# Strassen's algorithm for four of the seven pairs of token tiles in the last product of an attention and MoE kernel

## The chip, the cores and the metric

The kernel runs on one core of a Trainium2 chip. The metric is the time of one execution on the device, in microseconds (us). A core has TensorE (matrix products, PE in the profile, with its weight loads as PEld), VectorE (DVE), ScalarE (ACT) and GpSimd (POOL), each with its own row of instructions; SyncE (SP) and some of the others issue DMA transfers. An engine works its row off in order and waits, where it must, on semaphores.

## The reference, cut to what matters

```python
def _attn_ref(q, k, v, w_pre, w_post):           # 4 batches, 12 heads, 448 x 64
    scores = np.matmul(q, k.transpose(0, 1, 3, 2)) / np.sqrt(64)
    ...                                          # heads mixed, softmax, heads mixed
    return np.matmul(attn, v)

def _moe_ref(x, w_in, w_out, g_ln):              # x 1792 x 768, w_in 768 x 1024, w_out 1024 x 768
    h = x @ w_in
    e = np.exp(h - np.max(h, axis=-1, keepdims=True))
    solu = h * (e / (np.sum(e, axis=-1, keepdims=True) + 1e-9))
    mu = np.mean(solu, axis=-1, keepdims=True)
    var = np.mean((solu - mu) ** 2, axis=-1, keepdims=True)
    ln = (solu - mu) / np.sqrt(var + 1e-06) * g_ln
    return ln @ w_out
```

The result of the attention, 1792 token rows of 768, is x. The weights w_in and w_out come as fp64.

## The kernel before

The attention part fills the first 441 us or so and leaves x transposed in DRAM and, for the last batch, in SBUF. The change doesn't touch it. Then comes the part around the MoE layer, to which all that follows belongs. It works on 14 tiles of 128 token rows. Every factor of a product is held as two fp16 numbers, a higher and a lower half, and a product is three matmuls: high by high, high by low, low by high.

For each tile t:

- `hidden` (L984) is h = x @ w_in: 36 matmuls of 128x512, three products by six blocks of the inner dimension by two halves of the 1024 columns. The result lies in a pair of PSUM banks, `ps_h`, of which there are three (tile t uses number t modulo 3). The last batch's three tiles come first, from xsh and xsl, then those from xf0, xf1 and xf2, which SyncE loads from DRAM (L870, L872).
- On VectorE `solu_max` (L1508), on ScalarE `solu_exp` (L1519), on VectorE two steps on one column (`sm`, L1530 and L1533) and `solu_product` (L1536), behind which the bank pair is free for `hidden` of tile t + 3.
- The layer norm: `ln_mean` (nmu, L1547, VectorE), `ln_square` (L1552, ScalarE), `ln_var` (v, L1558, VectorE), `ln_root` (L1563, GpSimd, a power of -0.5), `ln_newton` in four small steps on VectorE (z, z again, rs, nm: L1568, L1571, L1574, L1578), `ln_apply` (L1584, GpSimd), and the split into a higher half `lh` (`ln_hi`, L1590, ScalarE) and a lower one `ll` (`ln_lo`, L1594, GpSimd).
- `turn` (L1598): SyncE issues two DMA transposes, from `lh` and `ll` in SBUF to `lth` and `ltl`, with nine slots each.
- `project` (L1609) is y = ln @ w_out: 48 matmuls of 128x384, eight blocks of the inner dimension by three products by two halves of the columns; each half has a PSUM bank. Tile 13 has 512 and 256 columns instead.
- `emit` (L1621, ScalarE) brings y to SBUF, and `stores` (L1765) go out on SyncE.

Beside the `hidden` tiles w_out is made ready. For each of its eight blocks of 128 rows SyncE fetches 768 KB of fp64 into one of two conversion buffers (`cv_wo`, L883), and six steps turn it into fp32: VectorE L898, ScalarE L901, VectorE L904, L909 and L914, GpSimd L917. ScalarE takes each block's maximum (`w_out_max`, L1478). When all eight are there, VectorE multiplies them with g (am_o, L1484) and reduces them; two matmuls on TensorE (`spread_wo`, L332) bring the maximum to all partitions; VectorE reduces it (L342), makes a power of two of it (L306 to L318) and `gs_wo` and `c_out` (L1490, L1491). Then ScalarE makes the eight higher halves `wo_h` (L360) and VectorE the eight lower ones `wo_l` (L365).

What stands where in an engine's row is decided by a planner: every piece of work is added with its engine and a cost, what it comes after, a due time and, if it takes a buffer, the ring of that buffer and what frees it. `moe.order()` then lists the pieces, by due times and modelled costs. `hidden` of tile t is due at 7.75 (t - 1), w_out's block kc at 9.0 kc, and `project` of tile t lags eleven tiles behind its `hidden`. In the list that results, TensorE's row is `hidden` 0 to 12, `project` 0, `hidden` 13, `project` 1 to 13.

Of the kernel before, what the change touches and what calls it, by code (L numbers as in the profile page):

```python
# [240 lines left out]
def kernel(  # L241
# [49 lines left out]
    E_S, E_X, E_LN = 19, 17, 10  # L291
# [1109 lines left out]
    with tc.manual_schedule():  # L1401
# [22 lines left out]
        lt_p = ctx.enter_context(tc.tile_pool(name="lt", bufs=9))  # L1424
# [20 lines left out]
        junk = wt_p.tile([128, DFF], F32, name="junk")  # L1445
# [20 lines left out]
        def fetch_w_out(kc):  # L1466
            fetch64(w_out[kc * 128 : (kc + 1) * 128], cv_p, "cv", DM, f"wo{kc}")
# [148 lines left out]

        def emit(t, n):
            if n == 0:
                outs[t] = h_p.tile([128, DM], F32, tag="o", name=f"o_{t}")
            c = slice(*ENDS[t][n : n + 2])  # L1620
            nc.scalar.activation(out=outs[t][:, c], in_=ys.pop((t, n)), func=AF.Copy, scale=c_out)  # L1621
# [12 lines left out]
        one = lambda f, *a: lambda e: f(*a)  # L1634
        add(("zf",), factors, {"dve": 2.2}, due=0.0)
        add(("zg",), lambda e: nc.sync.dma_start(out=g_sb, in_=g_ln.rearrange("(k p) -> p k", p=128)), {"sp": 0.6}, due=3.0, dma=(8, 4, 1))
        for kc in range(KFF):
            due = 9.0 * kc
# [6 lines left out]
                ring="cv",  # L1645
# [4 lines left out]
            on = ({"dve": 0.8}, {"act": 0.9}, {"dve": 1.25}, {"dve": 0.65}, {"dve": 1.35}, {"pool": 1.85})  # L1650
            for i in range(6):
# [6 lines left out]
                    due=due + 1.2 * i,  # L1658
                )
# [143 lines left out]
```

## Time and profile before

| | us |
|---|---|
| median of three runs (650.32 to 654.32) | 653.25 |
| span of the profiled execution | 657.9 |
| TensorE busy in it | 632.8 |
| VectorE busy | 475.1 |
| ScalarE busy | 451.0 |
| GpSimd busy | 280.1 |

The profiled execution is one run, recorded by instruction, and somewhat longer than the median. A busy time is the sum over the engine's instructions, overlaps counted once. An instruction's duration includes what it loses to another that it collides with, but not its wait for semaphores, which is the idle time before it. Times in the rows count from the start of the span.

### The profile page before, as it was taken

The numbers are of one execution on the slowest core, as the hardware profiler recorded it, in microseconds if no ns is written. First come the engines' busy times: TensorE is split into PE (matmuls) and PEld (weight loads), VectorE is DVE, ScalarE is ACT, GpSimd is POOL, SyncE is SP. The second block draws the span as 40 slices with busy tenths as digits, with TensorE's granted clock in tenths as the row PEclk, the third lists the DMA queues.
The fourth block names the chain that finished last, engine by engine and source line by source line (L and its number), as shares of the span: only waits on it lengthen the run. The fifth ranks groups of instructions, "written<-read, shape, count | busy, mean of one in ns | idle before, by whom it ended". The sixth has DMA issues, their size and how long they took to land.

```text
span 657.9 us, 17741 instructions
## 1 busy us (share of the span) xinstructions
PE 632.8 (96%) x6660; PEld 433.7 (66%) x6660; DVE 475.1 (72%) x1314; ACT 451.0 (69%) x981; POOL 280.1 (43%) x427
## 2 busy tenths in 40 slices
PE   6889999999999999999899999999999999999997
PEld 6647767777767778778677777774444455666664
DVE  5769998879997689997699999849889896100000
ACT  4679888989888898988799997725455576311111
POOL 2025683235844254593254246404666846300000
PEclk9779999999999999999899999999999999999999
DMA  9037578467677448788746763019964422541211
GB/s 242 12 133 229 178 152 178 156 196 221 204 185 169 150 140 236 234 175 206 219 154 221 214 224 119 3 41 295 186 160 112 97 48 57 113 113 51 64 55 48
DMA packets 114029, 98.53 MB, mean 150 GB/s; under 512 B 69604, under 2 KB 104600, under 8 KB 113944
## 3 DMA queue, kind: packets, MB, share of 16 engines
q1 hardware_dynamic: 108120, 83.62, 45.8%
q0 software_dynamic: 4416, 12.40, 6.9%
q10 hardware_dynamic: 1408, 1.38, 0.8%
q8 instruction: 52, 0.85, 0.5%
q14 instruction: 33, 0.27, 0.1%
HBM read 33.24 MB, written 9.63 MB: 65 GB/s over the span
## 4 chain that ended last, share of the span: by engine, by line
PE 64%; DVE 17%; ACT 7%; DMA 4%; issue 3%; POOL 2%; SPq 1%; ACTq 0%; DVEq 0%; POOLq 0%
PE y L1609 17%; PE po L766 15%; PE ps_h L984 12%; PE px L815 7%; PE ps L644 6%; PE pm L711 6%; DVE dead L721 4%; DVE s L661 3%; ACT e L737 3%; ACT s L656 2%; DMA raw_q<-in_q_dram 2%; DVE hl_k L365 1%; ACT p_t L369 1%; DMA sr<-s 1%; DMA cv_wi<-in_moe_w_in_dram 1%
## 5 line engine op out<-in xcount | busy, mean ns | idle before, releaser
L766 PE MATMUL po<-wr,e 128*112 128x120 f32 x1440 | 176.0, 273 | 6.4 <-POOL wr L758 4.9
L766 PEld LDWEIGHTS po<-wr,e 128*112 128x112 f32 x1440 | 156.8, 178 | 36.8 <-POOL wr L758 15.9
L758 POOL TENSOR_SCALAR wr<-wq,sm 128x120 f32<-128x120 f32 x180 | 77.1, 436 | 186.1 <-DVE sm L752 90.6
L737 ACT ACTIVATE e<-pm,nb,c_exp 128x448 f32<-128x448 f32 x180 | 131.4, 734 | 19.6 <-DVE dead L721 10.2
L721 DVE TENSOR_SCALAR_CACHE_REDUCE dead<-pm,c_nexp 128x448 f16<-128x448 f32 x180 | 121.7, 676 | 14.1 <-PE pm L711 10.1
L661 DVE SCALAR_TENSOR_TENSOR s<-ps,s 120x448 f16<-120x448 f32 (+1 forms) x192 | 112.2, 615 | 16.1 <-ACT s L656 13.8
L369 ACT COPY p_t<-po 112x480 f32<-112x480 f32 x180 | 108.2, 625 | 13.7 <-PE po L766 12.3
L656 ACT ACTIVATE s<-ps 120x448 f16<-120x448 f32 (+1 forms) x192 | 97.3, 552 | 18.1 <-PE ps L644 17.5
L815 PE MATMUL px<-p_t,raw_v 112*64 112x120 f32 (+3 forms) x1632 | 86.8, 259 | 0.8 <-ACT e L737 0.7
L815 PEld LDWEIGHTS px<-p_t,raw_v 112*64 112x64 f32 x1632 | 76.1, 137 | 16.0 <-issue 11.4
L984 PE MATMUL ps_h<-wi,xf 128*128 128x512 f16 x396 | 86.0, 379 | 0.2 <-DVE u L1536 0.2
L644 PE MATMUL ps<-k,q 64*64 64x448 f16 (+2 forms) x1008 | 79.7, 359 | 2.2 <-DVE s L661 1.5
L1609 PE MATMUL y<-wo_h,lth 128*128 128x384 f16 (+2 forms) x224 | 73.0, 326 | 0.0
L1609 PE MATMUL y<-wo_l,lth 128*128 128x384 f16 (+2 forms) x224 | 73.0, 326 | 0.0
L1609 PE MATMUL y<-wo_h,ltl 128*128 128x384 f16 (+2 forms) x224 | 73.0, 326 | 0.0
L984 PEld LDWEIGHTS <-xf 128*128 128x128 f16 x396 | 38.8, 98 | 46.8 <-issue 0.4
L1621 ACT ACTIVATE o<-y,c_out 128x384 f32<-128x384 f32 (+2 forms) x28 | 16.2, 579 | 72.7 <-PE y L1609 72.7
L1609 PEld LDWEIGHTS <-lth 128*128 128x128 f16 x448 | 43.8, 98 | 29.3
L711 PE MATMUL pm<-sr,wp_hi 64*64 64x448 f16 x720 | 57.1, 363 | 4.4 <-DMA sr<-s 2.4
L644 PEld LDWEIGHTS <-q 64*64 64x64 f16 (+2 forms) x1008 | 34.7, 107 | 24.4 <-issue 8.0
L1594 POOL TENSOR_TENSOR ll<-u,lh 128x1024 f16<-128x1024 f32 x14 | 31.4, 2245 | 15.1 <-ACT lh L1590 9.0
L737 ACT ACTIVATION_READ_ACCUMULATOR e<-pm,nb,c_exp 128x1 f32 x180 | 37.6, 209 | 0.0
(182 smaller groups left out, 800.1 us busy)
## 6 DMA issues: line engine op xcount, KB each, us to landing
sr<-s SPq DMA_DIRECT2D x176, 210.0 KB
cv_wi<-in_moe_w_in_dram SPq DMA_DIRECT2D x24, 256.0 KB
cv_wo<-in_moe_w_out_dram SPq DMA_DIRECT2D x8, 768.0 KB
raw_k<-in_k_dram POOLq DMA_DIRECT2D x18, 224.0 KB, 3.7
raw_q<-in_q_dram POOLq DMA_DIRECT2D x18, 224.0 KB, 5.4
raw_v<-in_v_dram POOLq DMA_DIRECT2D x18, 224.0 KB, 3.8
xh<-xsh SPq DMA_DIRECT2D x9, 224.0 KB
xl<-xsl SPq DMA_DIRECT2D x9, 224.0 KB
```

The lines of the kernel that those rows point to most:

```text
L369: nc.scalar.copy(out=out, in_=in_)
L644: nc.tensor.matmul(sps[b, c, h + e][lo:hi], q2[b, g][rows, 2 * j + x, i0 + lo : i0 + hi], k1[b, g][rows, 2 * j + y], start=(a == 0), stop= ...
L656: nc.scalar.activation(out=s_t[b, c][0 : y.shape[0], h, 0], in_=y, func=AF.Copy, scale=2.0**-E_S)
L661: nc.vector.scalar_tensor_tensor(out=t[:, h, 1], in0=y, scalar=2.0**-E_S, in1=t[:, h, 0], op0=ALU.mult, op1=ALU.subtract)
L711: nc.tensor.matmul(pmx[b, u + i][64 * e : 64 * e + 64, 0:S], w[rows], sr[b, u][rows, e, z], start=(a == 0), stop=(a == 2),)
L721: nc.vector.tensor_scalar(out=dead, in0=pmx[b, u][:, 0:S], scalar1=c_nexp[0:UK, b : b + 1], scalar2=None, op0=ALU.mult, op1=ALU.min, accum ...
L737: nc.scalar.activation(out=ee[b, u], in_=pmx.pop((b, u))[:, 0:S], func=AF.Exp, bias=nbs.pop((b, u)), scale=c_exp[0:UK, b : b + 1], accum_o ...
L758: ENG[eng].tensor_scalar(out=w, in0=wq[0:UK, 0 : H * UN], scalar1=sm, scalar2=1.0, op0=ALU.mult, op1=ALU.mult)
L766: nc.tensor.matmul(ps[:, c * 120 : (c + 1) * 120], e[:, c * CP : (c + 1) * CP], w, start=True, stop=True)
L815: nc.tensor.matmul(xps[b, blk, g][e * 64 : e * 64 + 64, i, cut], raws["v", b, p][:, e, c * D : (c + 1) * D], next(x for y, x in block_view ...
L984: nc.tensor.matmul(ps[:, n], xx[:, kc, o : o + 128], ww[:, kc, n * 512 : (n + 1) * 512], start=(kc == 0 and a == 0), stop=(kc == KDM - 1 a ...
L1609: nc.tensor.matmul(ys[t, n], lts[t, x][:, kc], w[:, kc, c0:c1], start=(kc == 0 and a == 0), stop=(kc == KFF - 1 and a == 2),)
```

## The change

The rows of the layer norm go through DRAM: `lh` and `ll` of a tile are stored there (L1662) and read back by a transposing DMA (L1674) into one tile `lt` per pair of token tiles. Such a pair tile has two slots of its own; two more are the places of xf1 and xf2, when `hidden` no longer reads these. All of y's products stand behind the last `hidden`. Pairs 0, 1 and 2 are computed as before, four results of 24 matmuls of 128x384. Pairs 3 to 6 use Strassen's algorithm in the form with few additions: the two tiles, the two halves of the inner dimension and the two halves of w_out's columns make a 2 x 2 by 2 x 2 product, which takes seven block products of 12 matmuls of 128x384 instead of eight. Their operands are sums and differences. Those of w_out are made once: it is scaled in place in fp32 (eight steps, ScalarE), `w_out_sum` (16 steps of 128x384, VectorE), and new halves `tz` in a former conversion buffer. Those of ln are made for each pair: `pair_whole` (two steps of 128x1024, VectorE, higher plus lower half in fp32, in the place of xf0 or of a raw buffer), `pair_sum` (four of 128x512, VectorE), `part_hi` (two of 128x1024, ScalarE), `part_lo` (two of 128x1024, VectorE). The seven products of a pair go in turn to six half banks of the three `ps_h` pairs, and `emit` adds them up: one step on ScalarE and nine on VectorE, of 128x384 from PSUM. A plain pair's `emit` runs on ScalarE or VectorE.

Also: the small steps nmu, v, the second z and nm move to ScalarE for all tiles; `junk`, into which `ln_square` writes, is fp16; the conversion of w_out has four buffers (two `cv`, two `sz`) and is due at 8.0 kc; the powers of two of ln and w_out change so that sums fit fp16; output stores go out on SyncE or on ScalarE's queue, from three buffers.

```diff
-    E_S, E_X, E_LN = 19, 17, 10
+    E_S, E_X, E_LN = 19, 17, 8
...
-        moe = Plan(h=3, u=3, lh=2, ll=2, th=9, tl=9, cv=2, X=1, Y=1, o=2)
+        moe = Plan(h=3, u=3, lh=2, ll=2, R=2, lt=2, x0=1, x1=1, x2=1, sz=2, B=6, tt=1, cv=2, X=1, Y=1, o=3)
...
+        def w_out_sum(k, i, eng):
...
+            b11, b12, b21, b22 = (raw_of(x)[:, n * DH : (n + 1) * DH] for x in (k, k + KH) for n in range(2))
+            out, x, y = ((t[:, 0], b12, b11), (t[:, 1], b22, t[:, 0]), (b21, b21, t[:, 1]), (b12, b22, b12))[i]
+            minus(eng, out, x, y)
...
-        def turn(t, z):
-            lts[t, z] = lt_p.tile([128, KFF, 128], F16, tag=f"t{z}", name=f"lt{z}_{t}")
-            nc.sync.dma_start_transpose(out=lts[t, z], in_=lns[t, z])
+        def ln_store(t, z, e):
+            QUEUE[e].dma_start(out=ln_dr["hl".index(z)][t], in_=lns[t, z])
...
+            nc.sync.dma_start_transpose(out=lts[i][:, z, t], in_=ln_dr[z][2 * i + t])
...
+        def pair_sum(i, j, eng):
+
+            a11, a12, a21, a22 = (xs[i][:, n] for n in range(4))
+            out, x, y, op = (
+                (a22, a21, a22, ALU.add),
+                (a21, a11, a21, ALU.subtract),
+                (a11, a22, a11, ALU.subtract),
+                (a12, a12, a11, ALU.subtract),
+            )[j]
+            ENG[eng].tensor_tensor(out=out, in0=x, in1=y, op=op)
...
+                y = ys[i, j] = bank(i, j)
+                terms = [(operand(i, j, z, k), factor(j, k)[n]) for k in range(KH) for z, n in ((0, 0), (0, 1), (1, 0))]
...
+            if j == 0:
+                nc.scalar.activation(out=px, in_=y, func=AF.Copy, scale=c_out)
+                return
+            work = {
+                1: lambda: [(py, px)],
+                3: lambda: [(px, px), (py, py)],
+                2: lambda: [(c(0, 0), px)],
+                4: lambda: [(c(1, 1), px), (px, px)],
+                5: lambda: [(c(1, 1), c(1, 1)), (c(1, 0), py)],
+                6: lambda: [(c(0, 1), px)],
+            }
+            for dst, x in work[j]():
+                nc.vector.scalar_tensor_tensor(out=dst, in0=y, scalar=c_out, in1=x, op0=ALU.mult, op1=ALU.add)
...
-            due = 9.0 * kc
+            due = 8.0 * kc
...
-                ring="cv",
+                ring=("cv", "sz")[kc % 4 // 2],
...
-                ("zm", ln_mean, {"dve": (0.08, 0.17)}, 4.1, None, None),
+                ("zm", ln_mean, {"act": (0.19, 0.29)}, 4.1, None, None),
...
-                ("zv", ln_var, {"dve": (0.1, 0.2)}, 5.6, None, None),
+                ("zv", ln_var, {"act": (0.19, 0.29)}, 5.6, None, None),
```

Three places in the new order are shown. The first is TensorE's row where w_out's maximum is spread. Before, the spread matmul stands between the last matmul of `hidden` 11 (bank ps_h_7620) and the first of `hidden` 12 (ps_h_7315):

```order
L984 MATMUL ps_h_7620<-wi_7289,xf_7756 128x512
L984 LDWEIGHTS xf_7756
L984 MATMUL ps_h_7620<-wi_7288,xf_7756 128x512
L332 MATMUL spread_wo<-ident_69,amx_wo 128x128
L984 LDWEIGHTS xf_7756
L984 MATMUL ps_h_7315<-wi_7288,xf_7756 128x512
```

After the change it stands one tile earlier, between `hidden` 10 (ps_h_7622) and `hidden` 11 (ps_h_7623):

```order
L984 MATMUL ps_h_7622<-wi_7289,xf_7774 128x512
L984 LDWEIGHTS xf_7774
L984 MATMUL ps_h_7622<-wi_7288,xf_7774 128x512
L332 MATMUL spread_wo<-ident_69,amx_wo 128x128
L984 LDWEIGHTS xf_7774
L984 MATMUL ps_h_7623<-wi_7288,xf_7774 128x512
```

So TensorE asks for the maximum one `hidden` tile sooner.

The second is VectorE's row at the end of w_out's conversion, up to am_o. Before, with the last conversion step (L914), the small steps of tile 8, and `solu_max` of tiles 9 (ps_h_7315) and 10 (ps_h_7619) around am_o:

```order
L909 TENSOR_SCALAR cv_wo_8288<-cv_wo_8288 128x768
L1558 TENSOR_SCALAR v_8379<-sq_8368,ch 128x1
L914 SCALAR_TENSOR_TENSOR cv_wo_8288<-cv_wo_8288 128x768
L1568 TENSOR_SCALAR z_8386<-y_8382,v_8379 128x1
L1571 TENSOR_SCALAR z_8386<-z_8386 128x1
L1574 TENSOR_SCALAR rs_8426<-z_8386,ch,y_8382 128x1
L1578 TENSOR_SCALAR nm_8430<-nmu_8365,rs_8426 128x1
L1508 TENSOR_SCALAR u_8432,nb_8433<-ps_h_7315,ch 128x1024
L1484 TENSOR_TENSOR am_o<-am_o,g_sb 128x8
L353 TENSOR_REDUCE amx_wo<-am_o 128x1
L1508 TENSOR_SCALAR u_8443,nb_8444<-ps_h_7619,ch 128x1024
```

After it, where L1559 is `solu_max`, L1587 `solu_product`, L1631 and L1637 the z and rs steps, and ps_h_7623 and ps_h_7315 are the banks of tiles 8 and 9:

```order
L909 TENSOR_SCALAR cv_wo_8080<-cv_wo_8080 128x768
L1637 TENSOR_SCALAR rs_8310<-z_8304,ch,y_8296 128x1
L914 SCALAR_TENSOR_TENSOR cv_wo_8080<-cv_wo_8080 128x768
L1631 TENSOR_SCALAR z_8318<-y_8312,v_8308 128x1
L1559 TENSOR_SCALAR u_8320,nb_8321<-ps_h_7623,ch 128x1024
L1637 TENSOR_SCALAR rs_8327<-z_8318,ch,y_8312 128x1
L1581 TENSOR_SCALAR sm_8329<-sm_8329 128x1
L1584 RECIPROCAL sm_8329<-sm_8329 128x1
L1587 SCALAR_TENSOR_TENSOR u_8320,su_8375<-ps_h_7623,sm_8329,u_8320 128x1024
L1559 TENSOR_SCALAR u_8378,nb_8379<-ps_h_7315,ch 128x1024
L1486 TENSOR_TENSOR am_o<-am_o,g_sb 128x8
L353 TENSOR_REDUCE amx_wo<-am_o 128x1
```

The conversion ends a whole `solu_max` and `solu_product` (tile 8's) sooner, the steps on one column are down to z and rs, and am_o no longer has tile 10's `solu_max` in front of the product of tile 9.

The third is SyncE's row in the `y` stage. Before, the transposes of the last tiles alternate with output stores:

```order
L1598 DMA_TRANSPOSE lth_8669<-lh_8561 128x8x128
L1598 DMA_TRANSPOSE ltl_8675<-ll_8572 128x8x128
L1765 DMA out_dram<-o_8623 80x768
L1765 DMA out_dram<-o_8623 48x768
L1598 DMA_TRANSPOSE lth_8818<-lh_8671 128x8x128
L1598 DMA_TRANSPOSE ltl_8823<-ll_8682 128x8x128
```

After it, with lt_8841 the tile of pair 2, lt_8902 of pair 3 and lt_8972 of pair 4:

```order
L1674 DMA_TRANSPOSE lt_8841<-ln_h 128x8x128
L1674 DMA_TRANSPOSE lt_8841<-ln_l 128x8x128
L1662 DMA ln_h<-lh_8893 128x1024
L1674 DMA_TRANSPOSE lt_8902<-ln_h 128x8x128
L1674 DMA_TRANSPOSE lt_8902<-ln_l 128x8x128
L1662 DMA ln_l<-ll_8898 128x1024
L1674 DMA_TRANSPOSE lt_8902<-ln_h 128x8x128
L1674 DMA_TRANSPOSE lt_8902<-ln_l 128x8x128
L2035 DMA out_dram<-o_8890 16x768
L1674 DMA_TRANSPOSE lt_8972<-ln_h 128x8x128
```

The transposes come in fours, a pair's at a time. The first of pair 2 waits until pair 0 is projected, since it takes that pair's slot, and the rest of the row stands behind it.

## Rows read from the trace of the kernel before

**Rows 1.** The page's head: busy us (share of span), instructions.

```profile
span 657.9 us, 17741 instructions
...
PE 632.8 (96%) x6660; PEld 433.7 (66%) x6660; DVE 475.1 (72%) x1314; ACT 451.0 (69%) x981; POOL 280.1 (43%) x427
```

**Rows 2.** Chain of waits, its end: start, us, engine, tile, line, count.

```profile
525.86 1.29 DVE u L1508 x2
...
528.80 7.93 PE ps_h L984 x36
...
544.53 7.77 PE ps_h L984 x36
552.30 101.41 PE y L1609 x624
...
653.73 0.47 ACT o L1621
```

**Rows 3.** TensorE's waits, 441 to 658: total us, times, longest.

```profile
PE ps_h L984 <- DVE u L1536: 0.2, 1, 0.2
```

**Rows 4.** Windows: length, busy PE, PEld, DVE, ACT, POOL; clock, DMA share, GB/s.

```profile
444.39:528.74 84.35, 84.18 (x392) 38.25 (x390) 73.98 (x152) 46.90 (x72) 54.48 (x35) 1.00 0.69 168
448.00:456.00 8.00, 8.00 (x39) 3.61 (x37) 7.41 (x17) 4.14 (x7) 3.88 (x3) 1.00 1.12 320
552.30:653.73 101.43, 101.40 (x624) 60.84 (x622) 6.17 (x20) 20.98 (x34) 10.70 (x8) 1.00 0.28 70
584.50:587.00 2.50, 2.50 (x17) 1.53 (x16) 0.00 (x0) 0.00 (x0) 0.00 (x0) 1.00 1.01 192
653.73:657.90 4.17, 0.00 (x0) 0.00 (x0) 0.00 (x0) 0.47 (x1) 0.00 (x0) 1.00 0.25 59
```

**Rows 5.** Lines, VectorE, 444.39 to 530.87: busy us, mean ns | idle before.

```profile
L1536 DVE SCALAR_TENSOR_TENSOR u<-ps_h,sm,u 128x1024 f32<-128x1024 f32 x11 | 14.1, 1284 | 0.4
L1508 DVE TENSOR_SCALAR_CACHE_REDUCE u<-ps_h,ch 128x1024 f32<-128x1024 f32 x11 | 14.0, 1275 | 0.7 <-PE ps_h L984 0.7
...
L1568 DVE TENSOR_SCALAR z<-y,v 128x1 f32<-128x1 f32 x9 | 2.4, 272 | 3.0 <-POOL y L1563 3.0
L1578 DVE TENSOR_SCALAR nm<-nmu,rs 128x1 f32<-128x1 f32 x9 | 1.9, 214 | 0.3
L1558 DVE TENSOR_SCALAR v<-sq,ch 128x1 f32<-128x1 f32 x9 | 1.9, 207 | 0.9 <-ACT junk L1552 0.8
...
L1547 DVE TENSOR_SCALAR nmu<-su 128x1 f32<-128x1 f32 x10 | 1.5, 148 | 0.2
L1571 DVE TENSOR_SCALAR z<-z 128x1 f32<-128x1 f32 x9 | 1.4, 154 | 0.3
L1484 DVE TENSOR_TENSOR am_o<-am_o,g_sb 128x8 f32<-128x8 f32 x1 | 1.1, 1118 | 0.6 <-ACT cv_wo L1478 0.6
```

**Rows 6.** Timeline of VectorE: start, us, line, operation.

```profile
450.29 0.96 DVE L914 SCALAR_TENSOR_TENSOR cv_wo<-cv_wo 128x768 f32<-128x768 uint32 x1
...
503.47 2.19 DVE L914 SCALAR_TENSOR_TENSOR cv_wo<-cv_wo 128x768 f32<-128x768 uint32 x1
...
530.79 0.61 DVE L342 TENSOR_REDUCE amx_wo<-spread_wo 128x1 f32<-128x128 f32 x2
...
532.34 0.15 DVE L1491 TENSOR_SCALAR c_out<-p_wo 128x1 f32<-128x1 f32 x1
```

**Rows 7.** Lines, all engines, 430 to 658, columns as in Rows 5.

```profile
L365 DVE SCALAR_TENSOR_TENSOR wo_l<-wo,gs_wo,wo_h 128x768 f16<-128x768 f32 x8 | 8.4, 1109 | 0.0
...
L1519 ACT ACTIVATION_READ_ACCUMULATOR u<-ps_h,nb,ch 128x1 f32 x14 | 2.7, 190 | 0.0
```

**Rows 8.** Timeline of SyncE's queue: start, us, line, operation.

```profile
463.43 3.24 SPq L1598 DMA_TRANSPOSE ltl<-ll x1
...
584.70 1.27 SPq L1598 DMA_TRANSPOSE ltl<-ll x1
```

**Rows 9.** The page's costliest groups: busy us, mean ns | idle before.

```profile
L661 DVE SCALAR_TENSOR_TENSOR s<-ps,s 120x448 f16<-120x448 f32 (+1 forms) x192 | 112.2, 615 | 16.1 <-ACT s L656 13.8
```

More of the change, by code (lines that the diff above doesn't have):

```diff
@@ L1617, in emit, with turn @@
[L1617 to L1621, printed above, removed]
+        def ln_store(t, z, e):
+            QUEUE[e].dma_start(out=ln_dr["hl".index(z)][t], in_=lns[t, z])
+        def turn(i, t, z):
+            if i not in lts:
+                n = i - NPL + 1
+                if 0 < n < B - 1:
+                    x = wt_p.tile(x_in[n].shape, F16, tag=f"xf{n}", name=f"lt_{i}")
+                    x = x.rearrange("p z k n -> p (z k n)")[:, 0 : 4 * DFF]
+                else:
+                    x = lt_p.tile([128, 4 * DFF], F16, tag="lt", name=f"lt_{i}")
+                lts[i] = x.rearrange("p (z t k n) -> p z t k n", z=2, t=2, k=KFF)
+            z = "hl".index(z)
+            nc.sync.dma_start_transpose(out=lts[i][:, z, t], in_=ln_dr[z][2 * i + t])
@@ new lines @@
+        T = TP
+        for n, (i, j) in enumerate(STEPS):
+            before = [STEPS[n - 1]] if n else []
+            a, b = 2 * i, 2 * i + 1
+            if i >= NPL:
+                ready = [("zT", i, int(j == 1), z) for z in "hl"] if j < 3 else [("zL2", i, int(j in (4, 5)))]
+                ready += [("zL", x) for x in range(*((0, 4), (12, 16), (4, 8), (8, 12), (8, 12), (16, 20), (4, 8))[j])]
+                ready += [("zp", NT - 1)]
+                ring, until = "B", [("zE", i, j)]
+            else:
+                ready = [("zT", i, PLAIN[j][0], z) for z in "hl"] + [("zL", k) for k in range(KFF)]
+                ring, until = "XY"[j % 2], [("zE", i, j)]
+            add(
+                ("zP", i, j),
+                one(project, i, j),
+                {"pe": TQ if i >= NPL else 2 * TQ},
+                after=ready,
+                behind=[("zP",) + x for x in before] or [("zh", NT - 1)],
+                due=T,
+                ring=ring,
+                until=until,
+            )
+            T += TQ if i >= NPL else 2 * TQ
+            last = i == NPP - 1
+            if i >= NPL:
+                ring = "o" if j in (2, 4) else None
+                t = a + (j == 4)
+                until = [("zO", t, x) for x in chunks(t)]
+                goes = {2: [(a, 0, 1)] if last else [], 5: [(b, 0, 2)], 6: [(a, int(last), 2)]}.get(j, [])
+                on = {"act": (0.45, 0.6)} if j == 0 else {"dve": (1.22, 1.35) if j in (3, 4, 5) else (0.61, 0.75)}
+            else:
+                t = a + PLAIN[j][0]
+                ring = "o" if j < 2 else None
+                until = [("zO", t, x) for x in chunks(t)]
+                goes, on = [(t, 0, 2)] if j > 1 else [], {"act": (0.58, 0.7), "dve": (0.55, 0.7)}
+            add(
+                ("zE", i, j),
+                lambda e, i=i, j=j: emit(i, j, e),
+                on,
+                after=[("zP", i, j)],
+                behind=[("zE",) + x for x in before],
+                due=T - 12,
+                ring=ring,
+                until=until,
+            )
+            for t, c0, c1 in goes:
+                cut = slice(c0 * DH, c1 * DH)
+                for x, (_, d, rows) in enumerate(stores(t, cut)):
+                    add(
+                        ("zO", t, x) + ((c1,) if c1 < 2 else ()),
+                        lambda e, d=d, rows=rows, t=t, cut=cut: QUEUE[e].dma_start(out=d, in_=outs[t][rows, cut]),
+                        {"sp": 0.6, "act": 0.6},
+                        after=[("zE", i, j)],
+                        due=T + 0.7 + 0.1 * x,
```

328 lines of the change are left out of this document (245 added, 83 removed).

## The prediction

> **What bounds the kernel now.** I read the page's head first: TensorE is busy 632.8 of 657.9 us [rows 1]. Then the end of the chain of waits: from 528.80 on it is TensorE alone, and just ahead of that a few VectorE steps stand in it; the waits give TensorE one idle time after 441.41, of 0.2 us, in front of the matmuls at 528.80 [rows 2, 3]. The windows say the same: in the last 101.43 us TensorE is idle for 0.03 us at clock 1.00, and VectorE works 6.17 us [rows 4]. So from 441 on the time is matmuls times their spacing, and other work counts only where it makes TensorE wait. Behind the last matmul lie 4.17 us. Up to the first `hidden` tile both kernels do the same work in the same order; I give that part nothing.
>
> **The sum, part by part.**
>
> *Matmuls.* After the last `hidden` tile 624 matmuls of 128x384 (48 of them cut into 512 and 256 columns, the same sum) take 101.41 us [rows 2], 0.1625 us each; tile 0's 48 lie ahead of that tile. All 14 tiles are 672. After the change three plain pairs take 96 each and four Strassen pairs 7 x 12 = 84 each, 624 in all. 48 go: 48 x 0.1625 = **7.80 us**. Tile and type of the new matmuls are the same, so I use the same spacing; the weight loads (60.84 us in that stretch [rows 4]) stay one to a matmul.
>
> The Trainium skill ("TensorE: Matmul & The Clock Gate", Back-to-back issue gap) says that a sustained stream of weight loads and matmuls settles at about 81 ns for 128 columns and 131 ns for 512, which is an estimate of 114 ns at 384; by it the 48 matmuls would be worth 5.5 us. This trace differs, with 162.5 ns at 384 and 216 ns at 512 (7.77 us for 36 [rows 2]), and the measurement decides.
>
> *The bank wait.* `hidden` 12 waits 0.2 us for tile 9's `solu_product`, because am_o and a `solu_max` stood ahead of it on VectorE [rows 2, 3]. With the conversion of w_out due earlier this goes: **0.2 us**.
>
> *`hidden` stage: does VectorE keep up?* The two spread matmuls of w_out's maximum now stand between `hidden` 10 and 11 instead of 11 and 12. One `hidden` is 7.77 us and `hidden` 11 ended at 528.6, so 10 ends at 520.8: by then am_o must be there. From 444.39 to 528.74 VectorE is busy 73.98 of 84.35 us [rows 4]. Up to am_o in its new place these go: one `solu_max` and one `solu_product` (2.6), nine or ten each of nmu, v, z' and nm, now on ScalarE (1.5 + 1.9 + 1.4 + 1.9), and a z and an rs step (0.5) that fall behind it [rows 5]. 64.2 are left, so am_o is done at 508.6 with no wait at all, and at 519.0 with all of today's 10.4 us of waits. It also stands behind tile 9's `solu_max`, which can't start before `hidden` 9 ends, at 513.0; 1.3 for that and 1.1 for am_o give 515.5 [rows 5, 6]. **Slack 2 to 5 us, cost 0.** Then comes tile 10's product, which must free its bank ahead of `hidden` 13: 520.8, 0.5 for the spread matmuls, 1.7 for the reductions and scale as from 530.79 to 532.49 today, 1.3 for a `solu_max`, six lower halves of w_out at 1.11, 1.1 of small steps, 1.3 for the product [rows 5, 6, 7]: 533.4. `hidden` 13 is due at 520.8 + 0.5 + 2 x 7.77 = 536.8. Slack 3. If that cover goes, each us late is a us.
>
> The small steps have no row on ScalarE; the nearest is its accumulator read of one column, 0.19 [rows 7]. Four a tile at 0.2 add 7 us to ScalarE's 46.90 of 84.35 [rows 4]: not a bound. They may lengthen a tile's chain by tenths, but behind the `solu_product` that TensorE waits for.
>
> *Rows through DRAM.* 28 stores of 256 KB are added on SyncE's queue, and the transposes now read DRAM. In the `hidden` stage this is at most 7.3 MB over 84 us, 87 GB/s beside today's 168; plain loads alone reached 320 [rows 4]. Cost 0.
>
> In the `y` stage SyncE works its instructions off in order. Pair 2's four transposes wait for the slot of pair 0, and pair 3's four stand behind them. Call the end of `hidden` 13 H. Pair 0 takes 96 x 0.1625 = 15.6 us, so they start at H+15.6, and pair 2 needs them at H+31.2. A transpose of today holds the queue for 1.27 us, at worst 3.24, and two of them keep the DMA engines for 2.5 us [rows 4, 8]; those read SBUF, and for DRAM there is no row. With T for one, pair 2 is in time up to T = (15.6 - 2.5) / 4 = 3.3. Pair 3 needs its sums at its fourth step, H+52.7: 8T, 2.5 for a store between and the landing, and 9.0 for two whole sums, four part sums, a cast and two lower halves (1.28, 0.64, 1.28, 1.28 each, worked out below; the cast is assumed as long as a VectorE step) must fit into 37.1 us: T = 3.2, and beyond it TensorE waits 8T - 25.6. I take T = 1.3, today's value where no loads of x or w_out run beside, as in the `y` stage: pair 3 is 15 us early. Cost 0, at the worst row 0.3.
>
> *VectorE in the `y` stage.* It was nearly empty; now it makes operands and recombines. Nearest prices: two-input steps of 768 columns in SBUF at 0.96 and 1.11 [rows 6, 7], so 1.28 to 1.48 for 1024 and 0.64 to 0.74 for 512; a step from PSUM with an added term 0.615 for 448 columns [rows 9], 0.53 for 384, at most 0.66. A Strassen pair has 4, 4 and 9 of these: 12.5 us, at most 14.8. TensorE needs 84 x 0.1625 = 13.65 a pair. Sums and lower halves of w_out add 16, plain emits and the rest of the chains 9. In all 75 us, at most 85, of 101.4; and pair 3's operands are made beside 46.8 us of plain matmuls, so the pairs start with a lead. **Cost 0**; if VectorE paced all four pairs at the bound, 4 x 1.15 = 4.6.
>
> *The end.* Today ScalarE's 0.47 and a store of 256 columns follow the last matmul, 4.17 us together [rows 2, 4]. After: VectorE's 0.53 and a store of 384 columns, on two queues. 0, within 0.5 either way.
>
> Sum: 657.9 - 7.8 - 0.2 = 649.9 us for a profiled run. The median of the runs is 653.25 where this execution has 657.9, so both scale by 0.993: **645.3**.
>
> **The rivals.**
>
> *A. VectorE is late in the `hidden` stage* (slack 2 to 5, and 3). For it: today's 10.4 us of waits may grow with ScalarE's load, and a w_out step that took 0.96 took 2.19 at another place [rows 6]. Against: 10 us of VectorE's work leave. Late by 2 to 6 beyond the slack: 647 to 651.
>
> The Trainium skill ("SBUF — State Buffer", SBUF: two separate sides) has a rule that fits those two rows: a VectorE step with two SBUF inputs and a GpSimd step that reads SBUF shut each other out for a whole instruction. By it the new two-input steps are slow too while GpSimd has work, some 20 us into the `y` stage, where VectorE has its lead.
>
> *B. VectorE paces the Strassen pairs.* For it: 12.5 to 14.8 a pair against 13.65. Against: the lead, and six banks. At the bound 4.6 us are lost: 648 to 650.
>
> *C. Transposes from DRAM are slow.* This ends on the other side: at 8T - 25.6 = 8, T = 4.2, the gain is gone, and at T = 5.0 the kernel is 1% slower; 653 to 662. Against it: the worst row today is 3.24, beside loads that the `y` stage lacks.
>
> *D. The matmuls saved are worth less than their spacing.* At 0.114 each, 647.7. Against: every shape of the stage sits at its spacing.
>
> **How the numbers follow.** Forecast 0.64 (644 to 647), A 0.15, B 0.10, C 0.06, D 0.05. The range from 643 to 651 leaves out most of C, the far ends of A and B (0.07) and an end better than counted (0.04). One per cent, about what a measurement of this kernel can tell from no change, is 6.5 us: under 646.7 is faster. Some 0.53 of the forecast's 0.64 lies there, and 0.02 of A; C and far ends make 0.07 slower; 0.38 lie within.
>
> **What would show it.** Right: 624 `y` matmuls, all behind `hidden` 13, in about 101.4 us, with no wait of TensorE over 0.3; `hidden` 13 ending 8.0 us earlier, since tile 0's `y` no longer stands ahead of it; the spread matmuls don't wait. A: TensorE waits for amx_wo or for tile 10's product. B: `y` of the fifth and later pairs waits for an emit or a lower half. C: the first Strassen pair waits for a transpose or a sum made of one, and SyncE's issues take over 3 us. D: a `y` stage under or over 101.4 us with no wait in it. It would also be wrong by a stall in the attention part, which both share, or by an end that grows by over 1 us.

## The result, and the profile after

| | before | after |
|---|---|---|
| median of four runs, us | 653.39 | 645.72 |
| lowest to highest | 650.32 to 654.32 | 645.40 to 648.39 |
| span of the profiled execution | 657.9 | 644.1 |

The ratio of after to before is 0.9898, with a 95% interval from 0.9869 to 0.9927. The forecast was 645.3. That the number came out almost to the tenth is luck: two terms of the sum were wrong, by 3.5 us together, and the start of the program, which the change doesn't touch, varies from run to run by as much.

The page's head of the kernel after, to be held against [rows 1]:

```profile
span 644.1 us, 17785 instructions
...
PE 619.3 (96%) x6612; PEld 425.6 (66%) x6612; DVE 542.9 (84%) x1361; ACT 471.3 (73%) x1046; POOL 280.3 (44%) x427
```

TensorE has 48 matmuls fewer, VectorE 67.8 us more work. The end of the chain of waits (start, us, engine, tile, line, count), which answers to [rows 2]:

```profile
550.60 0.54 DVE o L1764
...
551.18 31.45 PE y L1751 x192
582.63 54.61 PE ps_h L1751 x336
...
637.27 0.62 DVE o L1783
...
638.41 0.52 DVE o L1783
```

Two things are new in it. VectorE stands in the chain ahead of 551.18: TensorE waited there for an emit. And behind the last matmul there is not one step of VectorE but a row of them. The waits of TensorE from 430 on are one line, where [rows 3] had another:

```profile
PE y L1751 <- DVE o L1764: 0.6, 1, 0.6
```

The windows (length, busy PE, PEld, DVE, ACT, POOL, clock, DMA share, GB/s) of the `hidden` stage from the last attention matmul to the end of `hidden` 13, of the `y` stage, and of the end, which answer to [rows 4]:

```profile
431.71:535.00 103.29, 103.24 (x481) 46.84 (x480) 90.52 (x169) 71.98 (x140) 62.03 (x40) 1.00 0.59 175
535.00:637.24 102.24, 101.65 (x624) 60.85 (x622) 77.43 (x112) 33.77 (x57) 16.04 (x10) 1.00 0.52 121
637.24:644.10 6.86, 0.00 (x0) 0.00 (x0) 1.67 (x3) 0.00 (x0) 0.00 (x0) 0.73 0.34 86
```

The end took 6.86 us where [rows 4] has 4.17. To compare stages of two executions one needs a common mark. The last group of attention matmuls stands in both, before:

```profile
437.83 2.99 PE L815 MATMUL px<-p_t,raw_v 112*64 112x60 f32 x96
```

and after:

```profile
428.72 2.99 PE L815 MATMUL px<-p_t,raw_v 112*64 112x60 f32 x96
```

From the start of that group to the end of the span it is 657.9 - 437.83 = 220.07 us before and 644.1 - 428.72 = 215.38 after: **4.7 us less**, not 8.0. The other 9.1 us between the spans lie ahead of the mark, in instructions that both kernels share. Windows of the first stretches show where; before:

```profile
15.00:30.00 15.00, 11.88 (x124) 9.14 (x124) 10.23 (x29) 9.16 (x21) 0.00 (x0) 0.77 0.16 41
30.00:45.00 15.00, 13.44 (x121) 6.71 (x118) 10.57 (x27) 10.83 (x28) 2.76 (x10) 0.77 0.37 126
```

and after:

```profile
15.00:30.00 15.00, 13.54 (x148) 9.23 (x146) 12.68 (x36) 10.45 (x26) 0.25 (x2) 0.89 0.06 18
30.00:45.00 15.00, 11.48 (x147) 6.65 (x148) 11.55 (x29) 11.82 (x32) 5.77 (x15) 1.00 0.49 164
```

The granted clock was 0.77 in both stretches before, 0.89 and 1.00 after, and fewer matmuls were done there (245 against 295). By 50 us the profile of before is 5.2 us behind, instruction for instruction along VectorE's row. It stays so up to 309 us, and loses another 3.8 in one place; the same work of VectorE, before and after:

```profile
309.03:331.85 22.82, 20.38 (x240) 16.03 (x244) 16.60 (x46) 18.96 (x43) 7.14 (x12) 0.93 0.74 217
303.71:322.70 18.99, 18.65 (x244) 14.84 (x248) 16.82 (x46) 18.75 (x43) 7.41 (x12) 1.00 0.74 235
```

There VectorE waits 2.1 us for a load of w_in and then TensorE 2.4 us for another transfer, behind which its clock is 0.57 from 320 to 324.

### The profile page after: what moved, and what is told of

The parts are those of the page before. It is cut to its first block, busy times and chain, and to the rows that moved or that the text cites. A ratio compares the mean times of both kernels' runs of the same rounds, so it can differ in the third digit from the quotient of the medians.

```text
span 644.1 us, 17785 instructions
## 1 busy us (share of the span) xinstructions
PE 619.3 (96%) x6612; PEld 425.6 (66%) x6612; DVE 542.9 (84%) x1361; ACT 471.3 (73%) x1046; POOL 280.3 (44%) x427
## 4 chain that ended last, share of the span: by engine, by line
PE 62%; DVE 19%; ACT 7%; issue 4%; POOL 3%; DMA 3%; SPq 1%; DVEq 0%; ACTq 0%; POOLq 0%
PE po L766 15%; PE ps_h L984 13%; PE ps_h L1751 8%; PE px L815 7%; PE pm L711 6%; PE ps L644 6%; PE y L1751 5%; DVE dead L721 4%; DVE s L661 3%; ACT e L737 3%; DMA sr<-s 2%; ACT s L656 2%; DVE hl_k L365 2%; POOL wr L758 1%; DVE wo_l L365 1%
## 5 line engine op out<-in xcount | busy, mean ns | idle before, releaser
L656 ACT ACTIVATE s<-ps 120x448 f16<-120x448 f32 (+1 forms) x192 | 97.5, 554 | 16.4 <-PE ps L644 15.8
L1751 PEld LDWEIGHTS <-lt 128*128 128x128 f16 x432 | 42.3, 98 | 28.9 <-issue 1.0
L1751 PE MATMUL y<-wo_h,lt 128*128 128x384 f16 x192 | 47.2, 326 | 0.6 <-DVE o L1764 0.6
L1659 POOL TENSOR_TENSOR ll<-u,lh 128x1024 f16<-128x1024 f32 x14 | 33.3, 2379 | 11.4 <-ACT lh L1655 11.4
L711 PE MATMUL pm<-sr,wp_lo 64*64 64x448 f16 (+1 forms) x360 | 36.1, 349 | 0.0
L365 DVE SCALAR_TENSOR_TENSOR xsl<-px,x_sc,xsh 128x120 f16<-128x120 f32 (+1 forms) x96 | 25.9, 325 | 7.9 <-ACT xsh L360 7.9
L748 DVE TENSOR_SCALAR sm<-sm 128x2 f32<-128x2 f32 (+1 forms) x92 | 18.8, 204 | 15.1 <-ACT e L737 14.4
```

The costliest lines, as they stand in the source:

```text
L656: nc.scalar.activation(out=s_t[b, c][0 : y.shape[0], h, 0], in_=y, func=AF.Copy, scale=2.0**-E_S)
L711: nc.tensor.matmul(pmx[b, u + i][64 * e : 64 * e + 64, 0:S], w[rows], sr[b, u][rows, e, z], start=(a == 0), stop=(a == 2),)
L1751: nc.tensor.matmul(y, x, w, start=(n == 0), stop=(n == len(terms) - 1 ))
```

## The experiments

All times to the end are counted from the mark above, in each run's own profile:

| kernel | mark to end, us | last matmul to end | waits of TensorE behind the mark, us | ratio to before, 95% interval |
|---|---|---|---|---|
| before | 220.07 | 4.17 | 0.2 | |
| before again (e0) | 220.06 | 4.2 | 0.2 | 1.001 (0.9988 to 1.0032) |
| after | 215.38 | 6.86 | 0.6 | 0.9898 (0.9869 to 0.9927) |
| after again (e1) | 215.36 | 6.85 | 0.6 | 0.9936 (0.9913 to 0.9959) |
| after, third (e10) | 215.23 | 6.8 | 0.6 | 0.9918 (0.9889 to 0.9947) |
| e2, order of half banks | 212.91 | 4.4 | 0.6 | 0.9885 (0.9863 to 0.9907) |
| e3, all pairs plain | 220.34 | 4.9 | 0 | 1.0011 (0.9990 to 1.0032) |
| e4, e2 with five Strassen pairs | 210.23 | 4.4 | 0 | 0.9856 (0.9811 to 0.9900) |
| e5, e2 with plain emits on ScalarE | 212.06 | 4.4 | 0 | 0.9863 (0.9820 to 0.9906) |
| e6, small steps on VectorE | 218.96 | 6.9 | 3.6 | 0.9974 (0.9950 to 0.9998) |
| e7, each transpose twice | 276.5 | 6.5 | 9.5 in the `hidden` stage, 37.5 in the `y` stage | one run |
| e8, e2 with six Strassen pairs | 223.12 | 4.4 | 11.6 | 1.0042 (1.0023 to 1.0060) |
| e9, two conversion buffers | 216.01 | 6.8 | 1.4 | 0.9934 (0.9907 to 0.9962) |

The mark makes profiles comparable to 0.2 us, where the times of one kernel scatter over 5 to 7.

### Where the difference between 4.7 and 7.7 us comes from: e0, e1, e10

e0 is the kernel before, e1 and e10 are the kernel after, unchanged.

> The kernel before once more, unchanged. The two profiles differ in more than the change: counted from the same hidden matmul (441.41 before, 432.30 after) to the end, before takes 216.5 us and after 211.8, 4.7 less, while the times differ by 7.7 and the spans by 13.8. Theory 1 (the start of the attention part varies from run to run with TensorE's granted clock, 0.77 in two stretches before and 0.89 to 1.00 after; the change does nothing there): this profile has the same 216.5 +-0.3 behind that matmul, and ahead of it anything from 432 to 441, going with the clock of the first 60 us. Theory 2 (the change itself quickens the part ahead): ahead of that matmul it is again 3 to 9 us longer than in the kernel after, with the clock at 1.00 too.

> The changed kernel once more, for a profile and times on the same chip as the other three. Theory 1: 211.8 +-0.3 us from the same hidden matmul to the end, times 4.7 to 5.5 us below before if the starts are alike. Theory 2: times 7.5 us or more below.

> The changed kernel a third time, since its ratio to before was 0.990 and 0.994 in the two sets so far. Theory (4.2 to 4.7 us gained behind the first hidden matmuls, the rest is the start's clock): 0.992 to 0.995. Rival (7.7 us gained): 0.988 to 0.990.

The mark of e0:

```profile
430.74 2.99 PE L815 MATMUL px<-p_t,raw_v 112*64 112x60 f32 x96
```

650.8 - 430.74 = 220.06, to 0.01 us what it was, while the part ahead of the mark was 7.1 us shorter than in the first profile: 3.5 at the start, where its clock was 0.89 in both windows, and the rest in the stretch that took 22.82 us in the first profile and takes 19.01 here. In e1, the changed kernel, the part ahead of the mark took 433.24 us, with a clock of 0.77 in both of the first windows shown above. So the low clock of the start comes in both kernels, and theory 1 holds in the main: behind the mark the change is worth 4.7 us (0.9928 of 653.4), and the rest lies ahead of it, in what the change doesn't touch. The theory laid all of that rest on the start; in the first profile that stretch has 3.8 us of it. The three ratios, 0.990, 0.994 and 0.992, all hold 0.9928 in their intervals or miss it by 0.0001. The times alone don't rule out the rival of e10, since its interval reaches down to 0.9889; the mark does. Why the start's clock differs from run to run was not tried.

### The end: e2

```diff
-        return h_banks[n // 2][:, n % 2, 0:DH]
+        return h_banks[n % 3][:, n // 3, 0:DH]
```

> The seven products of a Strassen pair go to the six half banks in another order, so that two in a row lie in different ps_h pairs. Theory (the wait for a product is one for the whole ps_h pair, so each emit waits for the product after its own too, and three VectorE steps instead of one follow the last matmul): the emits of the last pair's sixth product start at its end, about 1.9 us ahead of the last matmul; one step of 0.6 us follows that, and the 6.9 us behind the last matmul become 4.5 to 5.7; 1.2 to 2.3 us faster than the kernel after. Rival (the end is set by the output stores, four in two queues of 0.7 us and their landing): behind the last matmul at most 0.5 us less. Second rival (a product now waits for an emit of the pair's other half): waits of TensorE in the Strassen pairs, and slower by these.

In the kernel after, the timeline of VectorE (start, us, line, operation, idle before and its end) closes like this:

```profile
633.37 1.14 DVE L1783 SCALAR_TENSOR_TENSOR xs<-ps_h,c_out,xs 128x384 f32<-128x384 f32 x2 [2.69 <-PE ps_h L1751]
...
637.27 0.62 DVE L1783 SCALAR_TENSOR_TENSOR o<-ps_h,c_out,o 128x384 f32<-128x384 f32 x1 [1.58 <-PE ps_h L1751]
637.80 1.13 DVE L1783 SCALAR_TENSOR_TENSOR o<-ps_h,c_out,xs 128x384 f32<-128x384 f32 x2
```

A product is 12 x 0.1625 = 1.95 us. The last pair's sixth ended at 637.24 - 1.95 = 635.3, but its two steps (`o<-o` and the first `o<-xs`) start at 637.27, with the seventh's. The fourth's two steps start at 633.37, when the fifth was done too. Each time it is the two products that share a `ps_h` pair: there is one wait for the whole pair, not for its half. In e2, where neighbours lie in different pairs:

```profile
638.38 0.62 DVE L1783 SCALAR_TENSOR_TENSOR o<-ps_h,c_out,o 128x384 f32<-128x384 f32 x1 [0.68 <-PE ps_h L1751]
638.91 0.61 DVE L1783 SCALAR_TENSOR_TENSOR o<-ps_h,c_out,xs 128x384 f32<-128x384 f32 x1
640.33 0.62 DVE L1783 SCALAR_TENSOR_TENSOR o<-ps_h,c_out,xs 128x384 f32<-128x384 f32 x1 [0.81 <-PE ps_h L1751]
```

The sixth product's steps start at its end, 1.9 us before the last matmul at 640.30, and one step is left behind that. The end went from 6.85 to 4.40 us, 2.45 less, a little more than the upper figure of the theory: 1.1 us are the two steps, and the rest is output stores that also started earlier. TensorE never waited for an emit of the other half. Both rivals fall.

### The wait in the `y` stage: e5

In e2's kernel:

```diff
-goes, on = [(t, 0, 2)] if j > 1 else [], {"act": (0.58, 0.7), "dve": (0.55, 0.7)}
+goes, on = [(t, 0, 2)] if j > 1 else [], {"act": (0.58, 0.7)}
```

> The order of half banks of e2_banks, and all emits of the plain pairs on ScalarE. Theory (the 0.6 us for which TensorE waits in the kernel after is a plain emit that stands on VectorE behind w_out sums, of which two took 2.3 us beside GpSimd's lower half instead of 0.55): no wait of TensorE in the y stage, 0.6 us less than e2_banks from the first y matmul to the last. Rival (ScalarE is late too, behind the casts of w_out's halves): a wait of the same size for an emit on ScalarE.

What made the emit late in the kernel after is seen on VectorE:

```profile
545.43 2.30 DVE L1511 TENSOR_TENSOR tt<-wo,tt 128x384 f32<-128x384 f32 x1
547.77 2.36 DVE L1511 TENSOR_TENSOR wo<-wo,tt 128x384 f32<-128x384 f32 x1
550.05 0.55 DVE L1511 TENSOR_TENSOR wo<-wo,wo 128x384 f32<-128x384 f32 x1
550.52 0.60 DVE L1764 TENSOR_SCALAR o<-y,c_out 128x384 f32<-128x384 f32 x1
```

and beside it on GpSimd:

```profile
544.95 4.77 POOL L1659 TENSOR_TENSOR ll<-u,lh 128x1024 f16<-128x1024 f32 x2
```

Two sums that take 0.55 us elsewhere took 2.3 while GpSimd subtracted its two lower halves, until 549.7. The emit stood behind them; its bank was asked for at 550.6 and free at 551.1. The Trainium skill ("SBUF — State Buffer", SBUF: two separate sides) has a VectorE step with two SBUF inputs and a GpSimd step that reads SBUF shut each other out for a whole instruction; these rows agree, with 2.3 us for a step whose own work is 0.55. In e5 the two sums took 2.30 and 2.38 us again, but no emit stands behind them, and the chain is TensorE alone:

```profile
536.51 46.80 PE y L1751 x288
583.31 54.61 PE ps_h L1751 x336
```

624 matmuls in 101.41 us, no wait: 0.8 us less than e2, where 0.6 was forecast. The wait cost more than its 0.58: in an unbroken row each matmul's record overlaps the one before it by 0.16 us, and across a wait it doesn't, so the matmul at 551.18 starts 0.74 us later than the spacing has it. The theory holds, and ScalarE was not late.

### What the Strassen pairs are worth: e3, e4, e8

e3 sets `NPL` to 7 and leaves out w_out's sums and scaled copies; e4 and e8 set it to 2 and 1 in e2's kernel.

```diff
-        NPP, NPL = NT // 2, 3
+        NPP, NPL = NT // 2, 7
```

> All seven pairs plain, with everything else of the change kept: 672 matmuls instead of 624, and without w_out's sums, the pair sums and their halves. Theory (48 matmuls at 0.1625 us are the whole gain): 7.8 us more than the kernel after from the first y matmul to the last, less the 0.6 us wait for the emit that stood behind w_out's sums, which goes; so 7.2 more, and 2 less behind the last matmul, about 5 us slower than after and as fast as before within 1. Rival (part of the gain comes from the four conversion buffers and the steps moved to ScalarE): clearly faster than before, by 2 us or more.

e3's chain has all of y in one row:

```profile
538.44 109.21 PE y L1751 x672
```

109.21 / 672 = 0.1625 us, as before, and the time is that of before (220.34 against 220.07 from the mark). The `hidden` stage is 0.4 us shorter than before, the end 0.7 longer. So without the 48 matmuls nothing is left of the gain: the four buffers and the moved steps bring none by themselves.

> The order of half banks of e2_banks, and five Strassen pairs instead of four (two plain ones). Theory (TensorE sets the y stage, and VectorE's 13.1 us a pair, as measured in the kernel after, fit under 13.65): 612 matmuls of y, 1.95 us faster than e2_banks. Rival (VectorE paces the pairs once its lead shrinks from 46.8 to 31.2 us of plain matmuls, with 25 us of w_out's sums and halves to make in it): waits of TensorE for a pair sum or a lower half of some 3 to 8 us in the first Strassen pair, so as fast as e2_banks or up to 6 us slower.

The chain of waits of e4 in the `y` stage, plain pairs and Strassen pairs:

```profile
537.80 31.20 PE y L1751 x192
569.00 68.26 PE ps_h L1751 x420
```

99.46 us for 612, no wait: 1.95 us from twelve matmuls, and 0.8 from the wait, which is gone here too; the emits stand at other places in VectorE's row. From the mark it is 2.7 us less than e2 and **5.1 less than the kernel after**, the best version of these: 0.9856 of before.

> The order of half banks of e2_banks and six Strassen pairs, one plain. With five there was no wait of TensorE in the y stage, and 612 matmuls took 99.46 us. Theory 1 (TensorE still sets the stage): 600 matmuls, 97.5 us, 1.95 us faster than e4_five. Theory 2 (VectorE paces the pairs: its lead is down to 15.6 us of plain matmuls, and w_out's sums and halves, some 25 us, must be done before the first Strassen product that needs them): waits of TensorE of 5 to 15 us at the first Strassen pairs, slower than e4_five by 3 to 13.

With six it turns. TensorE's waits:

```profile
PE ps_h L1751 <- ACT tz_h L1541: 8.4, 3, 4.3
PE ps_h L1751 <- DVE tz_l L1511: 3.2, 3, 1.7
```

The first Strassen pair waits for w_out's new halves, three times for a cast on ScalarE, which itself waits for VectorE's sums, and three times for the lower half on VectorE. The window of that stretch shows VectorE full; below it stands the whole `y` stage:

```profile
550.00:570.00 20.00, 8.39 (x42) 4.06 (x40) 19.50 (x31) 12.08 (x23) 6.87 (x5) 0.73 0.74 179
...
537.06:649.48 112.42, 100.81 (x600) 59.10 (x598) 97.77 (x143) 36.16 (x57) 17.90 (x11) 0.94 0.47 110
```

19.50 of 20 us. 223.12 against e4's 210.23 is 12.9 us more, where 1.95 less was to be had: 14.8 lost, 11.6 of it in waits. The rest is in the second line: TensorE is busy 100.81 us with 600 matmuls that take 97.5 at 0.1625. After it had begun to stand idle its granted clock fell to 0.50 (its level of 1.2 GHz) and stayed there from 560 to 572 us. Ten matmuls in a row start 0.32 us apart in it, which is 1.6 us; what is left lies around the six waits. Theory 2, VectorE as the bound, sets in with the sixth pair, and at the start of the row of pairs, not in its middle.

### The `hidden` stage: e6 and e9

e6 moves the four small steps back to VectorE; e9 gives the conversion of w_out two buffers.

```diff
-("zm", ln_mean, {"act": (0.19, 0.29)}, 4.1, None, None),
+("zm", ln_mean, {"dve": (0.08, 0.17)}, 4.1, None, None),
...
-("zv", ln_var, {"act": (0.19, 0.29)}, 5.6, None, None),
+("zv", ln_var, {"dve": (0.1, 0.2)}, 5.6, None, None),
...
-... {"act": (0.19, 0.29)} if i % 2 else {"dve": (0.17, 0.27)}, ...
+... {"dve": (0.17, 0.27)}, ...
```

> The kernel after with nmu, v, the second z and nm back on VectorE. In the kernel after am_o is there 5.6 us ahead of its spread matmul, and the product of tile 10 ends 2.6 us ahead of hidden 13. Four steps of 0.15 to 0.21 are 0.72 us a tile, 5.8 us for the eight tiles ahead of am_o, where VectorE has 6.4 us of waits to fill. Theory (the move is not what the time hangs on): no wait of TensorE over 0.5 us in the hidden stage, and the time of the kernel after within 1 us. Rival (the move is needed for am_o's earlier place or for hidden 13): TensorE waits 1 to 4 us for amx_wo or for the product of tile 10.

TensorE's waits in e6 behind the mark (total us, times, longest):

```profile
PE ps_h L984 <- DVE u L1587: 2.9, 2, 2.0
PE spread_wo L332 <- DVE amx_wo L353: 0.7, 1, 0.7
```

The rival holds. TensorE waits for am_o, and then twice for a `solu_product` late behind it, tile 8's and tile 10's. The `hidden` stage is 4.4 us longer (107.69 against 103.29); the `y` stage is 0.8 shorter, since the wait there is gone (101.41), so it is 3.6 us more from the mark. The theory had set the 6.4 us of VectorE's waits against the 5.8 us of added work and taken them for free; they were not. Which of them can't be filled was not tried, nor whether the steps would have to move if the spread matmuls stayed one tile later, as in e9 below.

```diff
-            p, n = ((cv_p, "cv"), (sz_p, "sz"))[kc % 4 // 2]
+            p, n = cv_p, "cv"
...
-                ring=("cv", "sz")[kc % 4 // 2],
+                ring="cv",
```

> The kernel after with two buffers for the conversion of w_out instead of four, due as in after. The spread matmuls then stand between hidden 11 and 12 again, as before the change. Theory (the buffers only bring w_out's maximum forward, and its lower halves and sums have room behind it): no wait in the hidden stage over 0.5 us, a y stage with at most 1 us more of waits; within 1 us of the kernel after. Rival (the earlier scale is needed for the sums of the first Strassen pair and for tile 10's product): waits of TensorE of 2 us or more.

TensorE's waits in e9 behind the mark:

```profile
PE y L1751 <- DVE o L1764: 1.4, 1, 1.4
```

No wait in the `hidden` stage; the spread matmuls are back between `hidden` 11 and 12. 0.6 to 0.8 us more from the mark, by a longer wait for a plain emit, the next one, behind a w_out sum that took 2.30: within the theory. To take them out of the changed kernel, one at a time, costs 0.7 us for the four buffers and 3.6 for the moved steps; e3 shows that neither gains anything without the Strassen pairs.

### Slow transposes: e7

```diff
-            nc.sync.dma_start_transpose(out=lts[i][:, z, t], in_=ln_dr[z][2 * i + t])
+            for _ in range(2):
+                nc.sync.dma_start_transpose(out=lts[i][:, z, t], in_=ln_dr[z][2 * i + t])
```

> The kernel after with every transpose issued twice into the same place, the second behind the first one's end, so that the time T for one rises from about 1.5 us to some 4 to 5. Theory (the bound of the prediction, TensorE waits 8T - 25.6 for the first Strassen pair's sums, and nothing below T = 3.2): at T = 4.5 a wait of about 10 us at the fourth product of pair 3, and some more at the next pairs. Rival (the transposes have more slack than that, since the next pairs' slots are free early): a wait under 3 us.

SyncE's timeline, pair 2's first and pair 3's last:

```profile
565.14 4.57 SPq L1675 DMA_TRANSPOSE lt<-ln_h  x2
...
602.50 4.89 SPq L1675 DMA_TRANSPOSE lt<-ln_l  x2
```

T was 5.3 us on the average of these eight, counted with what lies between. In the `y` stage TensorE waited:

```profile
PE ps_h L1752 <- DVE xs L1784: 15.8, 2, 10.9
PE y L1752 <- DVE o L1765: 14.2, 3, 6.9
PE ps_h L1752 <- DVE o L1784: 4.8, 1, 4.8
PE y L1752 <- DMA lt<-ln_l: 2.7, 1, 2.7
```

By 8T - 25.6 there would be a stall of 17 us at pair 3's fourth product. There is none at that product. TensorE had been held up before, at four places of the plain pairs (14.2 for emits, 2.7 for a transpose, 16.9 together), and behind it at three places for emits (20.6). VectorE's row shows why:

```profile
598.58 1.23 DVE L1690 TENSOR_TENSOR xs<-lt 128x1024 f32<-128x1024 f16 x1 [15.81 <-DMA lt<-ln_l]
599.72 0.61 DVE L1765 TENSOR_SCALAR o<-y,c_out 128x384 f32<-128x384 f32 x1
```

`pair_whole` (L1690) of the next pair waits for its transpose, and the emit of the pair being computed stands behind it. The same holds at pair 3's seventh product; the longest wait, 10.9, is for an emit behind one that waits 12.8 us for an output store, whose issue stands behind the transposes in SyncE's row. Another 12 us are busy time beyond 101.4 (113.45 for the same 624 matmuls), with the granted clock at 0.89 on the average of the stage. So slow transposes cost more than the rule says and by another path, and below which T they cost nothing was not measured. The `hidden` stage, where the prediction gave the rows through DRAM no cost, is 12.7 us longer here (115.96): loads of w_out stand behind transposes in SyncE's row, VectorE waits 6.9 us for them, and TensorE 8.7 for amx_wo. A kernel with transposes this slow is far slower than before (708.4 us in its one run), as rival C said, and by more than the 1% that C had for T = 5.0. In the kernel after they were not.

## Why the prediction was right, and where not

**What bounds the kernel.** Right. 101.65 of 102.24 us in the `y` stage and 103.24 of 103.29 in the `hidden` stage are TensorE.

**Matmuls, 7.80 us.** Right to the hundredth: 0.1625 us a matmul in each of e3, e4 and e5. e4's twelve fewer were worth 1.95 (101.41 to 99.46). At the 114 ns that the prediction estimated from the Trainium skill ("TensorE: Matmul & The Clock Gate", Back-to-back issue gap) they would have been worth 1.4; the runs don't agree with that.

**The bank wait, 0.2 us.** Gone, and the `hidden` stage is 0.39 us shorter (111.48 from the mark's end to `hidden` 13's end before, less 7.80 for tile 0's `y`, against 103.29). The term was small by half: across the wait `hidden` 12 also took 7.93 us instead of 7.77 [rows 2].

**VectorE in the `hidden` stage, cost 0.** Right, by slacks of the forecast size. am_o, which answers to a row of [rows 5], on VectorE's timeline:

```profile
505.31 0.16 DVE L1486 TENSOR_TENSOR am_o<-am_o,g_sb 128x8 f32<-128x8 f32 x1
```

The spread matmul stood at 511.3: 5.6 us of slack, where 2 to 5 were forecast. Tile 10's product ended at 524.5, `hidden` 13 began at 535.00 - 7.77 = 527.23: 2.7, where 3 were forecast. e6 shows that the cover is real: with the steps back it is gone, and the `hidden` stage is 4.4 us longer.

**Transposes, cost 0.** Right for this kernel. In the `y` stage they took 1.23 to 2.39 us of the queue, under the bound of 3.2 (up to 3.10 in the `hidden` stage, beside loads, with no wait of TensorE); the worst of the `y` stage on SyncE's timeline is

```profile
559.22 2.39 SPq L1674 DMA_TRANSPOSE lt<-ln_h  x1
```

They started at 550.63, H + 15.6, as forecast. The bound itself is not borne out: e7 has its waits at other places.

**VectorE in the `y` stage, cost 0.** Nearly. The total was 77.4 us, where 75 to 85 were forecast, and by form:

```profile
L1702 DVE TENSOR_TENSOR xs<-xs 128x512 f32<-128x512 f32 x16 | 11.0, 688 | 0.4
...
L1511 DVE TENSOR_TENSOR sz<-xs,sz 128x1024 f16<-128x1024 f32 x8 | 9.7, 1217 | 0.4 <-ACT sz L1707 0.4
L1783 DVE SCALAR_TENSOR_TENSOR o<-ps_h,c_out,xs 128x384 f32<-128x384 f32 x16 | 9.6, 612 | 4.6 <-PE ps_h L1751 4.6
L1689 DVE TENSOR_TENSOR xs<-lt 128x1024 f32<-128x1024 f16 x8 | 9.6, 1218 | 0.0
```

A pair is 4 x 1.22 + 4 x 0.69 + 9 x 0.61 = 13.1 us, between the 12.5 and 14.8 forecast and just under TensorE's 13.65. What failed is a detail: "some 20 us into the `y` stage, where VectorE has its lead" was true of the sums but not of the plain emits that stand behind them in the row, for which TensorE waits. That cost a wait of 0.58 us and 0.16 more across it. The prediction allowed no wait over 0.3.

**The end, "0, within 0.5 either way".** Wrong, the largest mis-sized term: +2.7 us, where the prediction itself had named an end that grows by over 1 us as a sign of being wrong. The step took it for granted that only the last product's emit follows the last matmul. Three steps did (1.67 us in the window against 0.47 in [rows 4]), and the stores behind them started later; e2 takes 2.45 of the 2.7 back. The kernel's text already had the two products in halves of one `ps_h` pair (`bank`); that one wait stands for both was seen only in the trace, where VectorE waits for TensorE ahead of the sixth product's emit and not again ahead of the seventh's.

**The sum.** Measured behind the mark: -7.80 + 0.81 in the `y` stage (0.74 of it the wait), -0.39 in the `hidden` stage, +2.69 at the end, -4.69; the profiles say 215.38 - 220.07 = -4.69. Without the two surprises (e5) it is 212.06 - 220.06 = -8.00, what the sum had said, though two small errors cancel in it: 0.2 more was gained in the `hidden` stage, and 0.2 lost at the end.

**Why the time came out at 645.7 all the same.** In the one execution of after that was profiled in that set the start was a good one, with the mark at 428.72, where the other profiles have it between 430.19 and 433.24, but for e10 (428.27) and the first of before (437.83). The starts of its three other executions aren't on record; two of them have its time within 0.4 us. In e1's set its median is 648.63 and the kernel before's 652.51, 4 us apart. The forecast of 645.3 lies in the range of times of the changed kernel, but its gain, 1.2%, is larger than what the change has: 0.7% by the mark, 0.6 to 1.0% by the three sets of runs.

**The rivals.** A and B didn't come. e6 shows A's mechanism, at the places named, one step of the change away. e8 shows VectorE as the bound, but at w_out's halves for the first Strassen pair, not at the later pairs that B names. C didn't come; e7 shows that slow transposes would be dear, by another path than C's. D fell with the spacing measured in e3, e4 and e5.

## What to carry to other kernels

When matmuls are cut on an engine that is full, the saving is, by these runs, count times spacing, as long as the other engines keep up (e8, one pair further, lost it all); what went wrong here was at the ends, so write out which steps must follow the last matmul, and read from the row of waits what each of them really waits for. Two results in halves of one buffer that are waited for as one make each consumer late by a whole product: put neighbours in different buffers. And compare stages from a mark that both programs share, since a varying start can hide or lend as much as the change is worth.

## What the runs showed of the hardware

- TensorE's granted clock between 15 and 45 us was 0.77 in one execution of the kernel after (e1) and 1.00 in another (e10), and everything behind came 5 us later in the first (the mark at 433.24 and 428.27). In the kernel before, 0.77 against 0.89 (e0) went with 3.5 us.
- After TensorE had waited 11.6 us in all for six operands (e8), its clock was 0.50 from 560 to 572 us, and matmuls of 384 columns in a row started 0.32 us apart there, 0.1625 elsewhere.
- A VectorE step with two inputs in SBUF, 0.55 us at 384 columns, took 2.30 and 2.36 while GpSimd subtracted in SBUF. am_o, on 8 columns, took 1.12 before [rows 5] and 0.16 after.
- A small step on one column costs 0.20 us on ScalarE (nmu) and 0.29 with a second operand (v, nm), against 0.15 and 0.21 on VectorE [rows 5].
